# Loading q and k one at a time from batch three on, with a larger attention lead and the constants split over two engines

## The chip, the cores and the metric

The kernel runs on one core of one Trainium2 chip. The metric is the device time of one execution in microseconds (us); the time before is about 306 us. A run is called fast when it is within 1.5% of the fastest run of the same kernel in the same job, and slow otherwise. Ratios are the mean time of one kernel's fast runs over that of the other's fast runs of the same rounds, so they are not quite the ratio of the medians that are quoted beside them.

Engine names in the profile: PE is TensorE's matmul, PEld its weight load, DVE VectorE, ACT ScalarE, POOL GpSimd, SP SyncE (which here only issues DMAs). The page and the views count from the start of the span.

## The reference

Causal attention with a decay that is summed along the sequence, then an MLP mixer over tokens and channels. There are 8 batches, 8 heads, 576 positions, 64 dimensions a head.

```python
def _attn_ref(q, k, v, s):                      # q, k, v: (8, 8, 576, 64), s: (8, 8, 576)
    scores = scale * np.matmul(q, k.transpose(0, 1, 3, 2))
    cum = np.cumsum(np.maximum(s, 0.0), axis=-1)
    bias = -(cum[:, :, :, None] - cum[:, :, None, :])
    scores = np.where(causal, -1000000000.0, scores + np.minimum(bias, 0.0))
    scores = scores - np.max(scores, axis=-1, keepdims=True)
    attn = np.exp(scores)
    attn = attn / (np.sum(attn, axis=-1, keepdims=True) + 1e-09)
    return np.matmul(attn, v)

def _moe_ref(x, w_tok1, w_tok2, w_ch1, w_ch2):  # x: (8, 576, 512)
    h = np.maximum(x.transpose(0, 2, 1) @ w_tok1, 0.0) @ w_tok2      # token mixer
    u = x + h.transpose(0, 2, 1)
    h2 = np.maximum(u @ w_ch1, 0.0) @ w_ch2                          # channel mixer, 1536 wide
    return u + h2
```

The kernel computes only a band of the attention and proves in passing that this is allowed. Part of the proof is a bound on the norms of q and k: ScalarE squares and sums every q and k tile. If the proof fails, a slow general path runs; with these inputs it does not.

## The kernel before

The whole program is unrolled. The kernel describes each piece of work as an operation with its engine, its guessed duration, and what it reads and writes. A planner, plain Python in the kernel, puts the operations in order by simulating them with those guesses. Each engine then executes its own list **in the planned order, and nothing is reordered at run time**. Semaphores make the waits correct; the guesses only decide the order.

The planner's rule for when a successor may start is the piece that the argument needs (most comments in the code cuts are added here):

```python
            for u in o.users:                 # o was just placed at est on engine e
                if u.after is o:
                    rdy = est + occ           # "after" only keeps the order: start when o has issued
                elif u.alts.keys() == {"PE"} and e == "PE":
                    rdy = est + occ
                elif e in u.alts and len(u.alts) == 1 and not o.dma:
                    rdy = est + occ
                else:
                    rdy = fin                 # for a DMA: when it has landed
```

The loads of q and k. One load brings four heads of one batch, 288 KB as written in bf16. GpSimd issues it (the data are cast on the way). The ring `qkn` has six buffers. A buffer is read twice: VectorE transposes it into `kT` or `qT` for the scores, and ScalarE squares it for the proof.

```python
    r_qn = ring("qkn", 6, [128, S * 2], BF16)
    ...
    def load_p(fn, key, us, n=1):             # all of GpSimd's DMAs form one chain by "after"
        lastp[0] = P.op({"POOL": (0.68 * n, 0, fn)}, writes=key, prio=1, dma=us, after=lastp[0])
    ...
    def load_quad(src, b, qd):
        n = Buf(r_qn)
        load_p(lambda: nc.gpsimd.dma_start(
            out=n.t[:, :], in_=src[b, 4 * qd : 4 * qd + 4, :, :].rearrange("g (p r) d -> (g p) (r d)", r=R)),
            [(n, 0)], 128 * 0.19 / 16)
        return n

    def square(n, col):                       # ScalarE, lowest priority
        P.op({"ACT": (1.2, 1.6, lambda: nc.scalar.activation(
            out=junk[:, :], in_=n.t[:, :], func=AF.Square, accum_out=sq[:, col : col + 1]))},
            reads=[(n, 0)], writes=[("sq", col)], prio=60)
    ...
    def stage_qk(b, qd, which=(0, 1)):
        for i, src in list(enumerate((k, q)))[which[0] : which[-1] + 1]:
            n = load_quad(src, b, qd)
            qkn[(b, qd, i)] = n
            if b >= 2:
                square(n, (b * 2 + qd) * 2 + i)

    def stage_sq(b, qd):                      # batches one and two are loaded again, only to be squared
        for i, src in enumerate((k, q)):
            square(load_quad(src, b, qd), (b * 2 + qd) * 2 + i)
```

Batches count from zero in the code, so `b >= 2` is batch three on. From batch three on, v is loaded from SyncE's queue, and the mixer's input is transposed by DMA (`uTa<-ua` and `uTb<-ub`), also from SyncE. `LAG` sets by how much the channel mixer of a batch stands behind attention in the priorities.

## Time and profile before

Before: 307.39 us median of the first three runs (303.72 to 307.66); 305.92 us with the later one of the same job. The profiled execution has a span of 304.4 us.

| part of the span | what limits it | read from |
|---|---|---|
| 0 to 15 us | start: loads, constants, first scores; TensorE is kept busy with matmuls on zeros | slices |
| 15 to 200 us | TensorE, without a gap | slices, windows |
| 200.9 to 206.7 us | one hole: DMA transposes of batch six are late | list of waits |
| 206.7 to 298 us | TensorE, the first 6 us at a low clock | windows |
| 298 to 304 us | last addition, store, end | chain |

The head of the page of before: busy time of each engine, then the span in 40 slices (a digit is the busy share in tenths; PEclk is the granted TensorE clock in tenths).

```profile
span 304.4 us, 6438 instructions
...
PE 290.0 (95%) x2588; PEld 163.7 (54%) x2588; DVE 190.0 (62%) x403; ACT 174.3 (57%) x291; POOL 45.7 (15%) x93
...
PE   7999999999999999999999999938999999999991
...
PEclk9999999999999999999999999996999999999997
```

The list of waits of before (engine, line, what it waited for: total us, times, longest). Three lines: the hole, and the waits of the squares for their loads.

```profile
ACT junk L586 <- DMA qkn<-in_k_dram: 14.8, 4, 5.5
...
ACT junk L586 <- DMA qkn<-in_q_dram: 7.5, 4, 4.0
...
PE pmx L920 <- DMA uTb<-ub: 5.8, 1, 5.8
```

Busy time by window in before. The columns are the window, its length, busy us of PE, PEld, DVE, ACT and POOL with instruction counts, then the granted clock, DMA share and GB/s.

```profile
45.00:60.00 15.00, 15.00 (x167) 8.52 (x164) 12.04 (x26) 13.18 (x21) 2.66 (x6) 1.00 1.16 228
60.00:80.00 20.00, 20.00 (x193) 12.77 (x192) 18.00 (x39) 18.21 (x32) 2.11 (x4) 1.00 1.06 227
80.00:100.00 20.00, 20.00 (x212) 11.37 (x210) 17.96 (x41) 11.39 (x19) 1.43 (x4) 1.00 0.76 135
100.00:120.00 20.00, 20.00 (x154) 9.88 (x152) 15.33 (x32) 14.09 (x23) 1.60 (x4) 1.00 0.82 177
120.00:180.00 60.00, 59.91 (x546) 32.48 (x545) 45.02 (x96) 32.74 (x52) 4.55 (x10) 1.00 0.56 108
...
206.70:212.50 5.80, 5.78 (x57) 3.16 (x58) 4.39 (x9) 4.03 (x6) 0.00 (x0) 0.58 0.21 81
```

TensorE is full in every window from 45 to 180 us, and between 60 and 80 us ScalarE is 91% busy as well. The last line shows the clock after the hole: 0.58 over 5.8 us.

The timeline of ScalarE in before, 49 to 62 us (start, duration, operation; in brackets idle time and its end). The `junk` lines are the squares of the loads; they stand **between** the exponentials (`E<-psc`) and the evictions of the mixer.

```profile
49.41 1.16 ACT L586 ACTIVATE junk<-qkn 128x1152 bf16<-128x1152 bf16 x1
...
53.85 1.93 ACT L681 ACTIVATE E<-psc 128x1024 bf16<-128x1024 f32 x2
...
57.33 1.15 ACT L586 ACTIVATE junk<-qkn 128x1152 bf16<-128x1152 bf16 x1
...
59.77 1.92 ACT L681 ACTIVATE E<-psc 128x1024 bf16<-128x1024 f32 x2
```

### The profile page before, as it was taken

To read this page: it belongs to the slowest core of one execution; us is meant where nothing else is said; L and a number is where in the kernel's file an instruction comes from. 1 tells how busy PE (TensorE), PEld (TensorE's weight loads), DVE (VectorE), ACT (ScalarE), POOL (GpSimd) and SP (SyncE) were. 2 spreads that over 40 slices of the span, in tenths; PEclk is the share of its full clock that TensorE was granted. 3 is DMA by queue.
4 is the path that set the end of the run, shared out by engine and by line. 5 is a ranking of instruction groups with operands and counts; after the bars stand their busy time and mean duration, and the time that the engine had idled before them with its cause. 6 is when DMAs were issued, how large, how long until landed. Compare 5 with 4: busy or idle time off the path is not lost.

```text
span 304.4 us, 6438 instructions
## 1 busy us (share of the span) xinstructions
PE 290.0 (95%) x2588; PEld 163.7 (54%) x2588; DVE 190.0 (62%) x403; ACT 174.3 (57%) x291; POOL 45.7 (15%) x93
## 2 busy tenths in 40 slices
PE   7999999999999999999999999938999999999991
PEld 2478855556755454457645455414764444457540
DVE  8674848788979966978867578956617333420020
ACT  3757878998872666538732688726862065018400
POOL 8984601210001010001001012200000000000000
PEclk9999999999999999999999999996999999999997
DMA  7999999999975995892228345993003410350032
GB/s 144 199 178 260 221 210 216 236 209 256 215 142 96 196 228 113 138 210 43 41 57 162 102 79 98 136 139 88 3 2 69 115 60 1 72 141 15 3 106 75
DMA packets 58341, 38.62 MB, mean 127 GB/s; under 512 B 44480, under 2 KB 47936, under 8 KB 58304
## 3 DMA queue, kind: packets, MB, share of 16 engines
q0 software_dynamic: 10128, 17.93, 34.7%
q1 hardware_dynamic: 48176, 20.21, 29.3%
q8 instruction: 22, 0.36, 0.5%
q14 instruction: 15, 0.12, 0.1%
HBM read 40.71 MB, written 9.44 MB: 165 GB/s over the span
## 4 chain that ended last, share of the span: by engine, by line
PE 86%; DMA 5%; POOL 3%; DVE 2%; issue 1%; ACT 0%; POOLq 0%; DVEq 0%
PE pmx L920 31%; PE pmx L938 29%; PE psc L657 6%; PE pmx L829 5%; PE pav L726 5%; PE pmx L798 5%; DMA uTb<-ub 4%; DMA vf<-in_v_dram 1%; PE psc L650 1%; POOL vf L553 1%; PE psc L726 1%; PE psc L798 1%; DVE gb L929 1%; POOL qkn L580 1%; PE pmx L832 1%
## 5 line engine op out<-in xcount | busy, mean ns | idle before, releaser
L920 PEld LDWEIGHTS <-wc 128*128 128x128 bf16 x624 | 59.1, 99 | 36.4 <-issue 6.9
L681 ACT ACTIVATE E<-psc 128x1024 bf16<-128x1024 f32 x61 | 59.8, 1022 | 31.3 <-PE psc L657 30.1
L920 PE MATMUL pmx<-uTb,wc 128*128 128x320 bf16 x384 | 57.8, 305 | 5.9 <-DMA uTb<-ub 5.8
L938 PE MATMUL pmx<-wc,gb 128*128 128x512 bf16 x240 | 54.9, 379 | 0.0
L586 ACT ACTIVATE junk<-qkn 128x1152 bf16<-128x1152 bf16 x32 | 37.2, 1161 | 22.5 <-DMA qkn<-in_k_dram 14.8
L938 PE MATMUL pmx<-wc,ga 128*128 128x512 bf16 x192 | 45.2, 379 | 0.0
L920 PE MATMUL pmx<-uTa,wc 128*128 128x512 bf16 (+1 forms) x240 | 44.9, 337 | 0.2 <-ACT uTa L870 0.2
L927 ACT ACTIVATE gb<-pmx 128x320 bf16<-128x320 f32 x72 | 31.1, 437 | 22.2 <-PE pmx L920 17.1
L927 ACT ACTIVATE ga<-pmx 128x512 bf16<-128x512 f32 (+1 forms) x53 | 26.7, 506 | 20.5 <-PE pmx L920 19.2
L938 PEld LDWEIGHTS <-gb 128*128 128x128 bf16 x240 | 22.6, 98 | 25.4 <-issue 0.3
L726 PEld LDWEIGHTS <-E 128*128 128x128 bf16 x576 | 24.6, 97 | 10.9 <-issue 1.5
L566 DVE TENSOR_TENSOR vp<-vf,wT 128x512 bf16<-128x512 f32 (+1 forms) x40 | 26.3, 682 | 4.3 <-DMA vf<-in_v_dram 4.1
L736 DVE TENSOR_TENSOR x<-pav,rc 128x320 bf16<-128x320 f32 x56 | 27.4, 490 | 1.7
L732 DVE RECIPROCAL rc<-pav 128x5 f32<-128x5 f32 x56 | 10.6, 189 | 28.7 <-PE pav L726 28.5
L938 PEld LDWEIGHTS <-ga 128*128 128x128 bf16 x192 | 17.8, 98 | 19.6 <-issue 0.8
L657 PEld LDWEIGHTS <-kT 32*128 32x128 bf16 x640 | 16.6, 94 | 16.4 <-issue 13.7
L726 PE MATMUL pav<-vp,E 128*128 128x65 bf16 x504 | 24.5, 193 | 0.0
L657 PE MATMUL psc<-qT,kT 32*128 32x256 bf16 (+2 forms) x608 | 24.1, 254 | 0.0
L580 POOL DMA_DIRECT2D qkn<-in_k_dram x20 | 10.8, 541 | 85.0 <-DVE E L697 28.0
L689 DVE TENSOR_TENSOR E<-E,keep 128x512 bf16<-128x512 bf16 x48 | 19.5, 410 | 3.0 <-ACT E L681 2.8
L829 PE MATMUL pmx<-h,w 128*128 128x512 bf16 (+1 forms) x82 | 21.1, 364 | 0.0
L952 DVE TENSOR_TENSOR of<-pmx,ub 128x512 f32<-128x512 f32 x16 | 11.0, 689 | 15.9 <-PE pmx L938 12.2
(105 smaller groups left out, 257.2 us busy)
## 6 DMA issues: line engine op xcount, KB each, us to landing
out_dram<-of SPq DMA_DIRECT2D x32, 256.0 KB, 3.1
vf<-in_v_dram SPq DMA_DIRECT2D x24, 256.0 KB, 6.7
qkn<-in_k_dram POOLq DMA_DIRECT2D x20, 288.0 KB, 6.2
qkn<-in_q_dram POOLq DMA_DIRECT2D x20, 288.0 KB, 5.8
vf<-in_v_dram POOLq DMA_DIRECT2D x8, 256.0 KB, 7.6
wc<-in_moe_w_ch_dram POOLq DMA_DIRECT2D x4, 384.0 KB, 9.3
wc<-in_moe_w_ch_dram POOLq DMA_DIRECT2D x3, 512.0 KB, 11.3
out_dram<-of SPq DMA_DIRECT2D x8, 128.0 KB, 2.4
```

Of the source, the lines that this page charges most:

```text
L566: eng.tensor_tensor(out=vp.t[p0 : p0 + n, c, :, 0:D], in0=vf.t[p0 : p0 + n, c, :, :], in1=wT[p0 : p0 + n, cw, b * H : b * H + H].unsqueeze ...
L586: P.op({"ACT": (1.2, 1.6, lambda: nc.scalar.activation(out=junk[:, :], in_=n.t[:, :], func=AF.Square, accum_out=sq[:, col : col + 1]))}, r ...
L657: nc.tensor.matmul(out=pss[g // 2].bank(g % 2)[:, o], lhsT=kT.t[rows, j0 : j0 + 128, e], rhs=qT.t[rows, a:z, e], start=(e == 0 and not fol ...
L681: nc.scalar.activation(out=E.t[:, :, gi * 512 : gi * 512 + 512], in_=ps.t[:, :, :], func=AF.Exp, scale=0.125)
L689: nc.vector.tensor_tensor(out=o, in0=o, in1=keep[:, :].unsqueeze(1).unsqueeze(1).to_broadcast([128, 2, 2, 128]), op=ALU.mult)
L726: nc.tensor.matmul(out=o[:, i, ic, 0 : D + 1], lhsT=E.t[:, hh, d0 : d0 + 128], rhs=vp.t[:, jc, h + hh, 0 : D + 1], start=(jc == j_lo), sto ...
L736: nc.vector.tensor_tensor(out=x.t[:, :, h0 * D : (h0 + n) * D].rearrange("p c (e d) -> p e c d", e=n), in0=view()[:, :, :, 0:D], in1=rc.t[ ...
L798: nc.tensor.matmul(out=pm()[:, (ha - h0) * D : (hb - h0) * D], lhsT=w1[:, NJ if odd and c == NJ - 1 else c, t * 128 : t * 128 + 128], rhs= ...
L829: nc.tensor.matmul(out=pm.t[:, 0 : e - a], lhsT=w2[:, t, w0 : w0 + 128], rhs=h1.t[:, t, a:e], start=(t == 0), stop=(t == NTC - 1 and b not ...
L920: nc.tensor.matmul(out=pm.t[:, 0 : e - a], lhsT=wc1[:, m, cc * 128 : cc * 128 + 128], rhs=uT.t[:, m, a:e], start=(m == 0), stop=(m == NMC ...
L927: lambda cc=cc, pm=pm, a=a, e=e: nc.scalar.activation(out=g.t[:, cc, a:e], in_=pm.t[:, 0 : e - a], func=AF.Relu),
L938: nc.tensor.matmul(out=pm.t[:, :], lhsT=g.t[:, cc, c * 128 : c * 128 + 128], rhs=wc2[:, cc, :], start=(cc == 0), stop=(cc == NCC - 1 and b ...
```

## The change

The intent. The hole at 201 us comes when q/k loads and DMA transposes share the DMA engines, so the change thins out the loads: GpSimd copies one element of the load before, which makes its queue wait until that load has landed. It also tells the planner that the DMA transposes land 1.2 us later than it believed, raises `LAG` from 2 to 3, makes the constants with two GpSimd selects and VectorE instead of GpSimd alone, splits the last output tile in two halves, and moves a few PSUM choices of batch one. The core of the diff:

```diff
+            o.slow = slow                                     # in op()
-                fin = dma_free + (1.5 if e == "POOL" else 0.9)
+                fin = dma_free + (1.5 if e == "POOL" else 0.9) + o.slow
...
-    LAG = 2.0
+    LAG = 3.0
...
+    nc.vector.memset(ident[:, :], 0.0)
+    nc.vector.memset(keep[:, :], 0.0)
     def consts():
-        make_identity(nc, identf)
-        make_identity(nc, ident)
-        make_upper_triangular(nc, keep, val=1.0, diag=True)
+        nc.gpsimd.affine_select(out=ident[:, :], in_=ident[:, :], ...)
+        nc.gpsimd.affine_select(out=keep[:, :], in_=keep[:, :], ...)
     def negs():                                               # negs2() likewise
-            nc.gpsimd.tensor_scalar(out=negm[:, a : a + w], in0=keep[:, 0:w], ...)
+            nc.vector.tensor_scalar(out=negm[:, a : a + w], in0=keep[:, 0:w], ...)
...
+    held = [None]
     def load_quad(src, b, qd):
         n = Buf(r_qn)
+        if held[0] is not None:
+            lastp[0] = P.op({"POOL": (0.12, 0.2, lambda h=held[0]: nc.gpsimd.tensor_copy(
+                out=gate[0:1, 0:1], in_=h.t[0:1, 0:1]))}, reads=[(held[0], 0)], writes=["held"], prio=1, after=lastp[0])
+        if b >= 2:
+            held[0] = n
         load_p(lambda: nc.gpsimd.dma_start(
...
                     P.op({"SP": (1.25, 0, trd)}, reads=rk, writes=[(uT, c, 0)],
-                         prio=0, dma=0.5)
+                         prio=0, dma=0.5, slow=1.2)
...
+            for (d0, d1) in ((0, DM // 2), (DM // 2, DM)) if last_c else ((0, DM),):   # last output tile in halves
```

Left out: the halved matmuls, additions and stores of that last loop, the order of v's first loads, and the PSUM choices.

The copy reads the load before (`reads=[(held[0], 0)]`): it waits until the load has landed.

More of the change, by code (lines that the diff above doesn't have):

```diff
@@ L57, in __init__, with op @@
         self.readers = {}
-    def op(self, alts, reads=(), writes=(), prio=0, dma=0.0, holds=(), after=None):
+    def op(self, alts, reads=(), writes=(), prio=0, dma=0.0, holds=(), after=None, slow=0.0):
         o = Op()
+        o.slow = slow
         o.alts = alts
@@ L366 @@
     FOLD = ((0, 0), (0, 1), (1, 0), (1, 1))
-    AV2 = ()
     PEADD = (0, 1)
@@ L441, in consts @@
     def consts():
-        make_identity(nc, identf)
-        make_identity(nc, ident)
-        make_upper_triangular(nc, keep, val=1.0, diag=True)
+        nc.gpsimd.affine_select(out=ident[:, :], in_=ident[:, :], compare_op=ALU.not_equal, fill=1.0, base=0,
+                                pattern=[[-1, 128]], channel_multiplier=1)
+        nc.gpsimd.affine_select(out=keep[:, :], in_=keep[:, :], compare_op=ALU.is_gt, fill=1.0, base=0,
+                                pattern=[[-1, 128]], channel_multiplier=1)
     def negs():
+        nc.vector.tensor_copy(out=identf[:, :], in_=ident[0:64, 0:64])
         for a, w in ((0, 128), (256, 128), (448, 64)):
-            nc.gpsimd.tensor_scalar(out=negm[:, a : a + w], in0=keep[:, 0:w], scalar1=30000.0, scalar2=-30000.0,
+            nc.vector.tensor_scalar(out=negm[:, a : a + w], in0=keep[:, 0:w], scalar1=30000.0, scalar2=-30000.0,
                                     op0=ALU.mult, op1=ALU.add)
@@ L452, in negs2 @@
         for a, w, k0 in ((0, 128, 0), (256, 128, 0), (448, 64, 64)):
-            nc.gpsimd.tensor_scalar(out=nego[:, a : a + w], in0=keep[:, k0 : k0 + w], scalar1=30000.0, scalar2=-30000.0,
+            nc.vector.tensor_scalar(out=nego[:, a : a + w], in0=keep[:, k0 : k0 + w], scalar1=30000.0, scalar2=-30000.0,
                                     op0=ALU.mult, op1=ALU.add)
     def load_consts():
-        lastp[0] = P.op({"POOL": (1.3, 1.5, consts)}, writes=["const"], prio=0, after=lastp[0])
-        lastp[0] = P.op({"POOL": (0.7, 0.9, negs)}, reads=["const"], writes=["negm"], prio=0, after=lastp[0])
+        lastp[0] = P.op({"POOL": (0.6, 0.8, consts)}, writes=["const"], prio=0, after=lastp[0])
+        P.op({"DVE": (0.5, 0.7, negs)}, reads=["const"], writes=["negm", "identf"], prio=-4)
+        P.op({"DVE": (0.4, 0.6, negs2)}, reads=["const"], writes=["nego"], prio=5)
     def pads(eng, i):
@@ L519, in w_tr @@
                                     identity=identf[:, :])
-        P.op({"PE": (0.7, 1.1, w_tr)}, reads=["wn", "const"], writes=[(bw, 0)], prio=(0,))
+        P.op({"PE": (0.7, 1.1, w_tr)}, reads=["wn", "identf"], writes=[(bw, 0)], prio=(0,))
         P.op({**dve(384, lambda: nc.vector.tensor_copy(out=wT[:, :, :].rearrange("p c e -> p (c e)"), in_=bw.t[:, 0:384])),
@@ L557, in stage_v @@
             else:
-                load_p(load, [(vf, c)], 1024 * 0.02 / 16 * n / 128, 1.5)
+                load_p(load, [(vf, c)], (0.75 if b or c == 0 else 1.25) * n / 128, 1.4)
                 yield
@@ L638, in quad @@
             fold = (b, qd) in FOLD
-            pss = [Duo() if b == 0 and qd * 4 + gi * 2 + e in (2, 5, 7) else Solo(r_sc) for e in range(2)]
+            pss = [Duo() if b == 0 and qd * 4 + gi * 2 + e in (2, 5) else Solo(r_sc) for e in range(2)]
             c0 = 0
@@ L709, in pair @@
         vkeys = [(vp, c) for c in range(NJ)] + [(vp, "w")] + (["padv"] if b == 1 else [])
-        for hs in ([(0, 1)] if b == 0 else [(0,), (1,)]):
-            pa = Solo(r_sc if b == 0 else r_mx if b in AV2 and hs[0] else r_av)
+        for hs in ([(0, 1)] if b == 0 and np_ != 1 else [(0,), (1,)]):
+            pa = Solo(r_sc if b == 0 and np_ != 1 else r_mx if b == 0 else r_av)
             rc = Buf(r_rc, False)
@@ L933, in chan @@
         for ci, c in enumerate((4, 0, 1, 2, 3) if odd else (0, 1, 2, 3)):
-            pm, o = Buf(r_mx, False), Buf(r_o, False)
-            for th in range(3):
-                def mm(c=c, pm=pm, th=th):
-                    for cc in range(th * 4, th * 4 + 4):
-                        nc.tensor.matmul(out=pm.t[:, :], lhsT=g.t[:, cc, c * 128 : c * 128 + 128], rhs=wc2[:, cc, :],
-                                         start=(cc == 0), stop=(cc == NCC - 1 and b not in OADD))
-                    if b in OADD and th == 2:
-                        sr, ii = (us, 0) if c == NJ - 1 else (u, c)
-                        nc.tensor.matmul(out=pm.t[:, :], lhsT=ident[:, :], rhs=sr.t[:, ii, :], start=False, stop=True)
-                P.op({"PE": (4 * c_pe(512)[0], 4 * c_pe(512)[0] + 0.3, mm)}, reads=gkeys + [("wc2", th)],
-                     writes=[(pm, 0)], holds=[o], prio=(rank + 2.0 + 2.0 * ci / NJ, 1))
+            o = Buf(r_o, False)
             if odd:
@@ L949, in chan @@
             sk = ukeys[(us, 0, 0)] + ukeys[(us, 0, 64)] if src is us else ukeys[(u, si, 0)]
-            def add(pm=pm, o=o, src=src, si=si):
-                nc.vector.tensor_tensor(out=o.t[:, :], in0=pm.t[:, :], in1=src.t[:, si, :], op=ALU.add)
-            if b in OADD:
-                P.op(either(512, lambda pm=pm, o=o: nc.scalar.copy(out=o.t[:, :], in_=pm.t[:, :]),
-                            lambda pm=pm, o=o: nc.vector.tensor_copy(out=o.t[:, :], in_=pm.t[:, :])),
-                     reads=[(pm, 0)] + sk, writes=[(o, 0)], prio=0)
-            else:
-                P.op(dve(512, add), reads=[(pm, 0)] + sk, writes=[(o, 0)], prio=0)
@@ L960, in st, with mm, add @@
-            def st(o=o, c=c):
-                if c < NJ - 1:
-                    nc.sync.dma_start(out=out[b, c * 128 : c * 128 + 128, :], in_=o.t[:, :])
-                else:
-                    for i in range(2):
-                        nc.sync.dma_start(out=out[b - 1 + i, NQ:S, :], in_=o.t[i * 64 : i * 64 + 64, :])
-            P.op({"SP": (0.45 if c < NJ - 1 else 0.9, 0, st)}, reads=[(o, 0)], prio=0.5, dma=128 * 0.088 / 16)
+            last_c = b == B - 1 and ci == NJ - 1
+            for (d0, d1) in ((0, DM // 2), (DM // 2, DM)) if last_c else ((0, DM),):
+                pm = Buf(r_mx, False)
+                for th in range(3):
+                    def mm(c=c, pm=pm, th=th, src=src, si=si, d0=d0, d1=d1):
+                        for cc in range(th * 4, th * 4 + 4):
+                            nc.tensor.matmul(out=pm.t[:, 0 : d1 - d0], lhsT=g.t[:, cc, c * 128 : c * 128 + 128],
+                                             rhs=wc2[:, cc, d0:d1],
+                                             start=(cc == 0), stop=(cc == NCC - 1 and b not in OADD))
+                        if b in OADD and th == 2:
+                            nc.tensor.matmul(out=pm.t[:, :], lhsT=ident[:, :], rhs=src.t[:, si, :], start=False, stop=True)
+                    occ = 4 * c_pe(d1 - d0)[0]
+                    P.op({"PE": (occ, occ + 0.3, mm)}, reads=gkeys + [("wc2", th)] + (sk if b in OADD and th == 2 else []),
+                         writes=[(pm, 0)], holds=[o], prio=(rank + 2.0 + 2.0 * ci / NJ, 1))
+                def add(pm=pm, o=o, src=src, si=si, d0=d0, d1=d1):
+                    nc.vector.tensor_tensor(out=o.t[:, d0:d1], in0=pm.t[:, 0 : d1 - d0], in1=src.t[:, si, d0:d1], op=ALU.add)
+                if b in OADD:
+                    P.op(either(512, lambda pm=pm, o=o: nc.scalar.copy(out=o.t[:, :], in_=pm.t[:, :]),
+                                lambda pm=pm, o=o: nc.vector.tensor_copy(out=o.t[:, :], in_=pm.t[:, :])),
+                         reads=[(pm, 0)] + sk, writes=[(o, 0)], prio=0)
+                else:
+                    P.op(dve(d1 - d0, add), reads=[(pm, 0)] + sk, writes=[(o, d0)], prio=0)
+                def st(o=o, c=c, d0=d0, d1=d1):
+                    if c < NJ - 1:
+                        nc.sync.dma_start(out=out[b, c * 128 : c * 128 + 128, d0:d1], in_=o.t[:, d0:d1])
+                    else:
+                        for i in range(2):
+                            nc.sync.dma_start(out=out[b - 1 + i, NQ:S, :], in_=o.t[i * 64 : i * 64 + 64, :])
+                P.op({"SP": (0.45 if c < NJ - 1 else 0.9, 0, st)}, reads=[(o, d0)], prio=0.5,
+                     dma=128 * 0.088 / 16 * (d1 - d0) / DM)
@@ L974 @@
     stage_qk(0, 1, (0,))
-    next(sv)
     load_consts()
     weights()
+    next(sv)
     stage_qk(0, 1, (1,))
@@ L986 @@
         load_ch1(1, m2)
-    if any(b == 1 for (b, qd) in FOLD):
-        lastp[0] = P.op({"POOL": (0.8, 1.0, negs2)}, reads=["const"], writes=["nego"], prio=0, after=lastp[0])
     for i in range(2):
```

## The prediction

> **What bounds it now.** TensorE: 290.0 of 304.4 us busy (the page's engine shares), full from 15 to 298 us except one hole. The list of waits names it: the channel mixer's first matmul on uTb waited 5.8 us for DMA uTb<-ub. There four q/k loads (issued 189 to 195 us, as buffers come free) share the DMA engines with batch six's five DMA transposes; these land 7 to 12 us after issue, against 2.4 alone. After the hole the granted clock is 0.58 from 206.7 to 212.5 us (the window table): 2.4 us more. This fits the Trainium skill, "TensorE: Matmul & The Clock Gate", Part 1: an idle window of about 3.4 us halves the clock. The hole costs about 8 us.
>
> **Gains.** (1) Hole: the eight late loads that only feed the norm check move ahead of those transposes: 6 to 8 us. They are not really throttled: all read the same, long landed tile. (2) Start: three memsets (0.6 us) and the -30000 masks (0.77 + 0.77 us) leave GpSimd; v's later issues come earlier: at most 1 us. (3) End: the last output is split; last add 0.69 to about 0.4 us, last store 3.1 to about 2.5: 0.5 to 1 us. Matmul columns are unchanged apart from 0.9 us more filler.
>
> **The cost.** The wait is a GpSimd copy reading the load before, in an in-order queue, so from batch three only one q/k load is in flight. In before, the first six such loads were in flight together behind the w_ch2 load; each took 12.4 to 14.6 us but they landed about 1.5 us apart, 45.7 to 53.6 us. The skill's "DMA: Bandwidth & Descriptors", Anatomy of one DMA, gives about 2.0 us fixed plus the transfer; serialized, the fixed part is paid each time. The trace agrees but is higher: a lone 288 KB load takes 3.6 to 3.8 us from issue to landing (140 to 180 us), 5.9 to 6.6 while the v loads run (45 to 89 us). With some 0.5 us for wait, copy and reissue, one load takes 4.2 to 6.8 us.
>
> That is on the critical path: ScalarE is in order and its squares of these loads stand between exponentials and evictions. The sixth load's square stands before batch three's second pair of exponentials: earliest 45.7 + 5 x 4.2 = 67 us, about 73 with v traffic; in before those ran at 59.8. The twelfth load (square at 79.8): earliest 92, likelier 100 to 106. ScalarE (91% busy, 60 to 80 us) and three PSUM buffers leave no slack, so TensorE stalls in pieces, some long enough to lower the clock. The larger attention lead makes these loads more urgent. From about 110 us loads are sparse and nothing is lost or regained.
>
> Sum (span): 304.4 - 8 (hole) - 1.5 (ends) + 22 (12 to 30) + 2 (clock) = 319; timed runs stand some 2 us above the span, within the error. **Predicted 319 us, 80% between 307 and 331. Faster 0.08, same 0.14, slower 0.78.**
>
> **What would show it.** GpSimd waiting on DMA qkn for most of 45 to 110 us, one q/k load every 4 to 7 us; squares waiting for DMA qkn over 15 us more in sum; TensorE below 80% busy in 50 to 110 us; that stretch's work ending 15 to 28 us later; the uTb wait under 2 us, the clock near 1.0 there.
>
> **What would make it wrong.** If loads land near 3.6 us despite v traffic, or TensorE has more slack than it seems, the loss shrinks to the gain: about 307; if the waits were not effective, about 296.

## The result

333.31 us median of 4 runs (331.73 to 334.06) against 305.92 us (303.72 to 307.66): the ratio is 1.0893, 95% interval 1.0794 to 1.0991. (As everywhere here, the ratio is the mean of the fast runs of one kernel over that of the other's fast runs of the same rounds, so not quite the ratio of the two medians.) The change makes the kernel 9% slower. The profiled run has a span of 330.0 us.

The head of the page after:

```profile
span 330.0 us, 6511 instructions
...
PE 296.0 (90%) x2605; PEld 167.0 (51%) x2605; DVE 195.2 (59%) x421; ACT 170.6 (52%) x284; POOL 51.2 (16%) x114
...
PE   6999997187967799879997999999999999999992
...
PEclk9999998769987999999999999999999999999998
```

The hole at 201 us is gone, and TensorE now has gaps from the seventh slice (50 us) to the 22nd (180 us). TensorE is busy for 6.0 us more although its matmuls are the same but for a few more on zeros (26 in the trace against 21, 0.3 us of busy time); the clock is lower in slices 7 to 13.

The list of waits after:

```profile
POOL gate L588 <- DMA qkn<-in_k_dram: 57.0, 12, 12.0
POOL gate L588 <- DMA qkn<-in_q_dram: 49.3, 12, 6.0
...
ACT junk L598 <- DMA qkn<-in_q_dram: 27.3, 9, 5.3
ACT junk L598 <- DMA qkn<-in_k_dram: 24.1, 9, 6.0
...
DVE qT L642 <- DMA qkn<-in_q_dram: 6.4, 3, 3.5
DVE kT L642 <- DMA qkn<-in_k_dram: 6.1, 3, 5.4
```

The squares now wait 51.4 us for their loads (27.3 + 24.1), against 22.3 us in before; VectorE's transposes wait 12.5 us. No wait on uTb stands in the list any more.

The same windows after:

```profile
45.00:60.00 15.00, 11.61 (x106) 7.03 (x101) 6.61 (x13) 4.79 (x10) 2.63 (x6) 0.89 0.93 185
60.00:80.00 20.00, 10.68 (x82) 5.28 (x82) 9.53 (x21) 11.65 (x18) 3.37 (x9) 0.74 0.55 96
80.00:100.00 20.00, 16.81 (x150) 10.26 (x149) 14.66 (x33) 11.34 (x20) 3.24 (x10) 0.90 0.89 170
100.00:120.00 20.00, 16.09 (x178) 10.07 (x177) 13.64 (x34) 13.03 (x21) 3.25 (x11) 0.93 0.56 96
120.00:180.00 60.00, 54.96 (x504) 29.20 (x503) 44.10 (x94) 31.36 (x47) 7.93 (x20) 1.00 0.69 138
...
200.00:220.00 20.00, 20.00 (x180) 9.91 (x180) 17.26 (x33) 13.59 (x20) 5.98 (x15) 1.00 0.73 137
```

Between 60 and 80 us TensorE is busy for 10.7 us of 20, at a mean clock of 0.74, and the DMA engines are half idle (share 0.55 against 1.06). So the DMA engines have room; the run with two loads in flight, below, tests whether a second load would use it.

GpSimd's timeline after shows one turn of the new loop: the copy waits for the landing, then the next load is issued.

```profile
60.16 0.18 POOL L588 COPY gate<-qkn 1x1 bf16<-1x1 bf16 x1 [6.36 <-DMA qkn<-in_k_dram]
60.67 0.54 POOL L592 DMA_DIRECT2D qkn<-in_q_dram  x1 [0.33 <-issue]
64.94 0.18 POOL L588 COPY gate<-qkn 1x1 bf16<-1x1 bf16 x1 [3.73 <-DMA qkn<-in_q_dram]
65.45 0.53 POOL L592 DMA_DIRECT2D qkn<-in_k_dram  x1 [0.34 <-issue]
```

And ScalarE's timeline after, at the place that was shown for before:

```profile
60.12 1.16 ACT L598 ACTIVATE junk<-qkn 128x1152 bf16<-128x1152 bf16 x1 [5.96 <-DMA qkn<-in_k_dram]
...
64.90 1.16 ACT L598 ACTIVATE junk<-qkn 128x1152 bf16<-128x1152 bf16 x1 [3.53 <-DMA qkn<-in_q_dram]
...
66.06 1.92 ACT L693 ACTIVATE E<-psc 128x1024 bf16<-128x1024 f32 x2
...
74.69 1.16 ACT L598 ACTIVATE junk<-qkn 128x1152 bf16<-128x1152 bf16 x1 [3.39 <-DMA qkn<-in_q_dram]
```

The first exponentials of batch three ran at 53.85 us before and run at 66.06 us now. In front of them stands the square of the fourth load, which waits for that load.

### The profile page after: what moved, and what is told of

It is laid out like the page before. It is cut to its first block, busy times and chain, and to the rows that moved or that the text cites. A ratio compares the mean times of both kernels' runs of the same rounds, so it can differ in the third digit from the quotient of the medians.

```text
span 330.0 us, 6511 instructions
## 1 busy us (share of the span) xinstructions
PE 296.0 (90%) x2605; PEld 167.0 (51%) x2605; DVE 195.2 (59%) x421; ACT 170.6 (52%) x284; POOL 51.2 (16%) x114
## 4 chain that ended last, share of the span: by engine, by line
PE 60%; DMA 23%; issue 7%; DVE 3%; ACT 3%; POOL 2%; POOLq 0%; ACTq 0%
PE pmx L958 25%; PE pmx L932 21%; DMA qkn<-in_q_dram 10%; DMA vf<-in_v_dram 5%; DMA qkn<-in_k_dram 5%; PE pmx L841 4%; PE pmx L810 4%; PE psc L669 3%; DMA wc<-in_moe_w_ch_dram 3%; PE pav L738 3%; ACT E L693 2%; ACT junk L598 1%; POOL qkn L592 1%; DVE gb L941 1%; DVE of L968 1%
## 5 line engine op out<-in xcount | busy, mean ns | idle before, releaser
L693 ACT ACTIVATE E<-psc 128x1024 bf16<-128x1024 f32 x62 | 60.8, 1021 | 39.0 <-PE psc L669 37.7
L932 PE MATMUL pmx<-uTb,wc 128*128 128x320 bf16 x384 | 59.3, 306 | 7.8 <-ACT gb L939 7.8
L598 ACT ACTIVATE junk<-qkn 128x1152 bf16<-128x1152 bf16 x32 | 37.2, 1163 | 51.4 <-DMA qkn<-in_q_dram 27.3
L958 PE MATMUL pmx<-wc,gb 128*128 128x512 bf16 (+1 forms) x252 | 54.6, 369 | 0.2 <-DVE ua L852 0.2
L958 PE MATMUL pmx<-wc,ga 128*128 128x512 bf16 x192 | 47.6, 398 | 0.0
L939 ACT ACTIVATE gb<-pmx 128x320 bf16<-128x320 f32 x70 | 30.0, 437 | 22.8 <-PE pmx L932 18.5
L958 PEld LDWEIGHTS <-gb 128*128 128x128 bf16 x252 | 23.6, 98 | 24.7 <-issue 0.8
L958 PEld LDWEIGHTS <-ga 128*128 128x128 bf16 x192 | 18.7, 102 | 22.3 <-issue 4.1
L939 ACT ACTIVATE ga<-pmx 128x512 bf16<-128x512 f32 (+1 forms) x47 | 23.3, 506 | 12.3 <-PE pmx L932 11.5
L642 DVE STREAM_TRANSPOSE kT<-qkn 128x576 f32<-128x576 f32 x16 | 20.0, 1252 | 8.4 <-DMA qkn<-in_k_dram 6.1
L588 POOL COPY gate<-qkn 1x1 bf16<-1x1 bf16 x31 | 8.1, 260 | 106.4 <-DMA qkn<-in_k_dram 57.0
L642 DVE STREAM_TRANSPOSE qT<-qkn 128x576 f32<-128x576 f32 x16 | 20.0, 1248 | 6.5 <-DMA qkn<-in_q_dram 6.4
```

Source lines behind the costliest of these rows:

```text
L598: P.op({"ACT": (1.2, 1.6, lambda: nc.scalar.activation(out=junk[:, :], in_=n.t[:, :], func=AF.Square, accum_out=sq[:, col : col + 1]))}, r ...
L642: P.op({"DVE": (1.24, 1.4, lambda n=n, dst=dst: nc.vector.transpose(out=dst.t[:, 0:S, :].rearrange("d t e -> d (t e)").bitcast(FP32).rearr ...
L693: nc.scalar.activation(out=E.t[:, :, gi * 512 : gi * 512 + 512], in_=ps.t[:, :, :], func=AF.Exp, scale=0.125)
L932: nc.tensor.matmul(out=pm.t[:, 0 : e - a], lhsT=wc1[:, m, cc * 128 : cc * 128 + 128], rhs=uT.t[:, m, a:e], start=(m == 0), stop=(m == NMC ...
L939: lambda cc=cc, pm=pm, a=a, e=e: nc.scalar.activation(out=g.t[:, cc, a:e], in_=pm.t[:, 0 : e - a], func=AF.Relu),
L958: nc.tensor.matmul(out=pm.t[:, 0 : d1 - d0], lhsT=g.t[:, cc, c * 128 : c * 128 + 128], rhs=wc2[:, cc, d0:d1], start=(cc == 0), stop=(cc == ...
```

## The experiments

The theory: in a fixed order, one load in flight cannot bring the tiles as early as ScalarE's and VectorE's lists ask for them, and every late tile stops TensorE. Rivals: the larger lead or the moved constants spoil the order; the copies delay other work in GpSimd's queue; one load at a time is too slow in any order.

Medians below are of all runs of a kernel. Before ran in every job: medians 306.10, 305.78 and 306.33 us, single runs from 300.03 to 311.48. In the job of the first four runs before's fastest run was 300.03 us, so only the few runs near it count as its fast ones and the ratios of that job are rough (their intervals say so); there the medians are the better guide. Before also spreads more than the kernels without the hole (`e_nowait`: 299.99 to 301.26), and its mean clock differs from run to run (0.998 in the run of 300.03 us, 0.992 or less in the others of that job). So the hole is perhaps not the same in every execution; only one execution of before was profiled, so this is not shown.

### The wait alone, and all but the wait

Two edits. `e_nowait` is the changed kernel without these lines:

```diff
-        if b >= 2:
-            held[0] = n
```

> The changed kernel without the wait: q/k loads are issued as buffers come free, everything else of the change stays. Theory (the one-at-a-time loads cost the time, and the rest of the change gains a little): 295 to 301 us, no TensorE hole over 2 us between 45 and 180 us. Rival (the larger attention lead or the moved constants made the order of work worse, and the waits only show it): 320 us or more.

`e_waitonly` is the kernel before with the copy (the same five added lines of `load_quad` as in the change) and nothing else.

> The kernel before with the wait alone added, lead 2, old constants, old tail. Theory: 325 to 337 us, squares waiting for DMA qkn in 45 to 120 us as in the changed kernel. Rival (larger lead and new order are to blame): 303 to 310 us.

Measured: without the wait 300.67 us median (299.99 to 301.26; ratio 0.9964, interval 0.9819 to 1.0108); the wait alone 336.00 us (334.71 to 337.82; ratio 1.112, interval 1.0938 to 1.1303). Both as the theory said. The lead and the constants are not to blame: the whole loss comes with the wait, and without it the change is about 5 us faster than before by the medians (the interval of the ratio does not exclude a tie). In the wait alone the squares wait 53.7 us for their loads (34.5 + 19.2), and the wait does not even close the hole that it was meant for. This line stands in the list of waits of `e_waitonly`:

```profile
PE pmx L927 <- DMA uTb<-ub: 3.8, 1, 3.8
```

Without the wait no such line is left. So something else in the change closes the hole. In `e_nowait` the last q/k load is issued at 190.5 us, before batch six's first transpose at 193.8 us; in before two of those loads were issued after the first transpose. Which of the edits brought this order was not tested alone.

The run without the wait executes the same instructions in the same order on every engine as the changed kernel, apart from the copies. So the two traces can be laid side by side. Its list of waits has no single wait of TensorE over 2 us, and its windows are full again; these are two of them:

```profile
60.00:80.00 20.00, 20.00 (x201) 12.39 (x201) 17.76 (x43) 16.76 (x28) 2.11 (x4) 1.00 1.04 217
80.00:100.00 20.00, 19.85 (x229) 11.98 (x229) 19.50 (x48) 14.64 (x22) 1.43 (x4) 1.00 0.74 134
```

The spans are 298.7 and 330.0 us: the wait costs 31.3 us. TensorE is busy 288.6 and 296.0 us. So 7.4 us of the 31.3 are the same matmuls taking longer, and 23.9 us are gaps.

### Two in flight

The same wait, on the load before the last one, so that two are in flight:

```diff
-    held = [None]
+    held = [None, None]
...
-            held[0] = n
+            held[:] = [held[1], n]
```

> The changed kernel, where each load waits for the one before the last: two in flight. Theory (it is the rate of loads): a load every 2.3 to 3.5 us, the sixth lands by 60 us and the twelfth by 78 us, so ScalarE's waits on DMA qkn fall below 20 us in sum and the time is 296 to 305 us. Rival (any wait in GpSimd's queue delays, through the small copies for v' that stand in the same queue): still 315 us or more.

Measured: 299.38 us median (299.05 to 300.31). But this edit changes two things. The copy now reads one load and stands `after` another, so the planner's rule gives it the landing: the planner now knows of the wait and orders the work accordingly. The next run takes that away again, with the copy held to the buffer instead of reading it in the planner's books (the copy itself, and its wait on the chip, stay):

```diff
-  reads=[(held[0], 0)], writes=["held"], prio=1, after=lastp[0])
+  holds=[held[0]], writes=["held"], prio=1, after=lastp[0])
```

> Two loads in flight, the planner not told (same order on ScalarE, VectorE and TensorE as in the changed kernel and in the run without the wait; in the first run with two in flight the planner happened to know of the wait, so that run changed two things). Theory (the rate of loads against a fixed order): a load every 2.5 to 3.3 us from 46 us, sixth load landed at 57 to 61 us (its square was at 56.8 without the wait, 74.4 with one in flight), twelfth by 74 to 79 us (78.3 and 105.9): 300.5 to 305 us. Rival (in the first run with two in flight the gain over one came from the planner's knowledge, as in the run where it knew of single loads): 312 us or more.

Measured: 304.12 us median (303.16 to 305.43). This kernel has the same order on TensorE, VectorE, ScalarE and SyncE as the changed kernel and as the run without the wait, so three kernels differ only in the number of loads in flight. The start of some squares on ScalarE, in us, from the timelines:

| square of load | buffers the only limit (`e_nowait`) | two in flight (`e_two_blind`) | one in flight (after) | after minus first |
|---|---|---|---|---|
| 1 (batch three) | 47.27 | 47.95 | 47.02 | -0.3 |
| 4 | 51.68 | 53.68 | 64.90 | 13.2 |
| 6 | 57.03 | 60.51 | 74.69 | 17.7 |
| 12 (batch five) | 78.56 | 81.63 | 106.16 | 27.6 |
| 18 | 109.91 | 111.48 | 140.24 | 30.3 |
| 22 (batch eight) | 145.21 | 147.66 | 176.50 | 31.3 |
| median time of the kernel | 300.67 | 304.12 | 333.31 | 32.6 |

The delay of the last column ends at the difference of the spans, 31.3 us. Going through ScalarE's instructions one by one in the two traces, every step of the delay of 0.8 us or more stands at a square. Two in flight take away nine tenths of the loss at the same order. That settles the rival of the copies too: this kernel has the same kind of copies in the same queue.

### One in flight, but the planner knows

The changed kernel, with the copy no longer tied to the load by `after`, so that the planner sees the landing. The loads are still one at a time.

```diff
-  reads=[(held[0], 0)], writes=["held"], prio=1, after=lastp[0])
+  reads=[(held[0], 0)], writes=["held"], prio=1)
```

> The changed kernel, where the kernel's own planner is told that the copy waits for the landing (the same loads, still one at a time; only the planned order of the other engines follows it). Theory A (the cost is an order planned as if the wait took no time; with the wait known the four loads of a batch need 4 x 4.5 = 18 us of about 33 us a batch): 299 to 310 us. Theory B (one load at a time is too slow for the kernel in any order): 320 us or more, with the same sum of waits on DMA qkn.

Measured: 305.32 us median (305.10 to 307.38). Theory A. GpSimd waits almost as long as in the changed kernel (47.3 + 44.5 us, against 57.0 + 49.3 us), but the squares wait only 9.2 us (6.6 + 2.6) instead of 51.4 us. From its list of waits:

```profile
POOL gate L588 <- DMA qkn<-in_k_dram: 47.3, 10, 11.7
POOL gate L588 <- DMA qkn<-in_q_dram: 44.5, 11, 5.7
...
ACT junk L598 <- DMA qkn<-in_k_dram: 6.6, 6, 3.0
...
ACT junk L598 <- DMA qkn<-in_q_dram: 2.6, 3, 1.2
```

The loads come no earlier: the twelfth lands at 116.3 us here and at 106.1 us in the changed kernel. Only the order around them is another. One load at a time is nearly fast enough for this kernel; it is not fast enough for an order that was planned as if the wait took no time. What is left of the gap to 300 us is largely a new idle stretch of TensorE of 3.2 us between 200 and 220 us, which I did not follow further.

### Which reader carries the delay

The squares only serve the proof. They were taken out for batches three to eight (the proof is then incomplete; `sq` is zeroed, and the output of these inputs is right).

```diff
-            if b >= 2:
-                square(n, (b * 2 + qd) * 2 + i)
```

> The changed kernel, waits kept, but without ScalarE's squares of batches three to eight (the norm check is then incomplete on purpose; the output of these inputs does not need it). In the changed kernel the loads reach VectorE's transposes 9 to 10 us later than in before (fourth to eighth load), but reach the squares up to 27 us later (twelfth load: lands at 106 us, squared at 78.5 to 79.8 us in before). Theory S (the squares, in ScalarE's order ahead of exponentials and evictions, carry most of the delay): 306 to 316 us. Theory T (the transposes need the loads as late anyway): 322 us or more.

Measured: 313.94 us median (313.21 to 315.20; ratio 1.0302, interval 1.0244 to 1.0361). So of the 32.6 us between the medians of the changed kernel and the run without the wait, 19.4 us go away with the squares and 13.3 us stay. What stays is most likely the transposes that the scores need, which wait 13.9 us for loads there (7.1 + 6.8). Most of the delay passed through work that could have been done at any time, only because it stands in an in-order list. Caution: without the squares the planner also finds a somewhat different order, and ScalarE has 24 squares of 1.16 us less to do, which by itself may save time, so the split is not exact.

### The wait from batch five on

```diff
-        if b >= 2:
+        if b >= 4:
```

> The changed kernel with the wait from batch five on in place of batch three: 8 of the 24 waits fewer, and the first eight loads are issued as buffers come free. Theory (the loss is a lead that is lost while w_ch2 and the first v loads fill the queues, 45 to 80 us, after which one load per 4.5 us would keep up): 298 to 305 us. Rival (one load at a time is too slow at any stage): 312 us or more.

Measured: 308.92 us median of four runs, 304.45 and 307.78 us for the two that count as fast (ratio 1.004, interval 0.9958 to 1.0123). Between the two ranges, so both statements missed. Letting the first eight loads go free takes away most of the loss, but not all: one load at a time still costs some 4 to 7 us in the fast runs against 300.67 us.

### The lead and the start

The old lead of 2, without the wait:

```diff
-    LAG = 3.0
+    LAG = 2.0
```

> The changed kernel without the wait and with the old lead of 2: what the larger lead does by itself, beside the run without the wait (300.67 us median). If the lead matters to the hole before batch six's channel mixer: 303 us or more, with a uTb wait of over 2 us; if only the planner's longer landing time for transposes closed it: 299 to 302 us.

Measured: 301.65 us median (300.87 to 302.61; ratio 0.9900, interval 0.9845 to 0.9956), and no wait on uTb. The lead is not what closed the hole, and it is worth about 1 us at most.

Two in flight with the old constants (the memsets and masks back on GpSimd, the old order of v's first loads):

> Two loads in flight as in the earlier run (299.38 us median), with the constants made as in before (GpSimd memsets and masks, old order of v's loads). In the runs without the wait the first channel mixer matmul started at 27.3 us against 26.1 in before: theory, the new start costs about 1.2 us, so 297.7 to 298.7 us here; rival, the first 30 us do not set the end: 299 to 300 us.

Measured: 299.84 us median (299.17 to 301.82; ratio 0.9849, interval 0.9801 to 0.9897): no difference to the new constants that these runs can tell. The test was less clean than planned. The first channel mixer matmul started at 28.26 us here, against 27.57 us with the new constants and no wait and 26.33 us in before, so the old constants alone do not bring back the earlier start of before. The theory's 297.7 to 298.7 us was missed.

### The hole of the kernel before

The eight loads that only feed the proof (`stage_sq`) were left out of the kernel **before**, again incomplete:

```diff
-    for b in range(2):
-        for qd in range(2):
-            stage_sq(b, qd)
```

> The kernel before without the eight q/k loads of batches one and two that only feed the norm check (incomplete on purpose). Theory (the hole of 5.8 us before batch six's channel mixer, with the low clock after it, comes from these loads standing in front of its DMA transposes): no wait on uTb over 1 us, clock 1.00 in 200 to 220 us, 296 to 300 us. Rival (the transposes are late because of the output stores or the order of work): the hole stays, 303 us or more.

Measured: 298.60 us median (298.25 to 298.73; ratio 0.9800, interval 0.9728 to 0.9871). The wait for DMA uTb is down to 0.2 us in sum, and the windows that held the hole are full, at full clock:

```profile
200.00:206.70 6.70, 6.70 (x81) 4.48 (x80) 5.74 (x13) 4.02 (x7) 0.00 (x0) 1.00 0.31 98
206.70:212.50 5.80, 5.80 (x66) 4.43 (x64) 2.81 (x9) 3.94 (x9) 0.00 (x0) 1.00 0.01 3
```

In before, the five DMA transposes between 190 and 202 us took 7.3 to 11.8 us from issue to landing. Here they take 2.5 to 4.0 us. The hole goes with those loads, so the reading that the change starts from was right. The run also takes eight squares off ScalarE (1.16 us each) and lets the planner order the rest anew, which these numbers do not separate.

### A version that beats both

Two loads in flight, with the planner knowing, once more with five rounds:

> The first run with two in flight and the planner knowing, again, for the comparison and as the version to keep: 299 to 300.5 us, beside 304 to 307 us of before.

Measured: 299.56 us median (299.10 to 300.09), before 306.33 us; ratio 0.9829, interval 0.9776 to 0.9882. Its squares wait 8.7 us for loads (5.0 + 3.7), the transposes under 1 us, and no wait on uTb is in its list. It is a little over 2% faster by the medians and 1.7% by the ratio of fast runs; at a threshold of 2% that verdict is unclear. It is the best complete kernel, ahead of the run without any wait by 1.1 us between the medians of two jobs, which is too little to claim.

## Why the prediction was right or wrong

It said slower with 0.78, and the kernel is slower; but 333.3 us lies outside 307 to 331 us. The mechanism was right and terms of the sum were mis-sized: in spans, the profiled run took 330.0 us where the sum said 319. Of these 11 us, some 7 are a loss that was put too low (24 for 31.3 us) and some 4 a gain that was put too high (9.5 for 5.7 us).

- **What bounds before: right.** TensorE and one hole. The run without the eight loads shows both the cause of the hole and its worth: 306.33 to 298.60 us, 7.7 us, where I wrote "about 8 us" (that run also dropped eight squares, as said there).
- **Gains of 9.5 us (8 for the hole, 1.5 for the ends): too high.** Everything but the wait brought the span from 304.4 to 298.7 us, 5.7 us. The end gained about 0.4 us: 6.4 us from the last matmul to the end of the span in before, 6.0 us without the wait. The start gained nothing: the first channel mixer matmul came at 27.57 us, 1.2 us later than in before. Why it came later stays open: with the old constants and two loads in flight it came at 28.26 us.
- **One load takes 4.2 to 6.8 us: right.** From the second load's issue at 46.12 us to the thirteenth's at 106.71 us there are 11 turns, 5.5 us each on average. The first two took 7.1 and 7.4 us, above the range, and the other nine 5.1 us on average, so the middle of the range was met partly by luck.
- **When the tiles come: right within 2 us.** I expected the sixth load's square at "about 73" and the twelfth's likelier at "100 to 106" us. In the changed kernel they started at 74.69 and 106.16 us.
- **The loss of "22 (12 to 30)" + 2 us: this is the step that failed. It measured 31.3 us.** Two faults. First, I did not draw the conclusion from my own line above. The twelfth square at 100 to 106 us against 79.8 us is a delay of 20 to 26 us (and 79.8 us was a miscount: in before that is the eleventh square, the twelfth ran at 81.77 us); the right comparison was the same order without the wait, where that square stands at 78.56 us, so the delay is 27.6 us. I wrote 22. Second, "From about 110 us loads are sparse and nothing is lost or regained" is false by half: nothing was regained, but the delay grew from 27.6 to 30.3 us at load 18 and to 31.3 us at load 22. The order leaves almost no slack between landing and square there even without the wait (in `e_nowait` the square of load 18 starts 0.1 us after its landing), so any later landing shows in full.
- **The low clock: named, but counted too low.** I put 2 us. TensorE's busy time grew by 7.4 us against the run without the wait, with a mean clock of 0.74 between 60 and 80 us. The gaps alone, 23.9 us, are close to the 22 us of the sum. TensorE's account (gaps and longer matmuls) and the delay of the squares are two ways to count the same 31.3 us, so the clock should not have been a term of its own: in the list of ScalarE's instructions the delay grows by steps of 0.8 us or more only at squares that wait for a load, and the slow matmuls run between them.
- **Signs.** GpSimd waiting on DMA qkn for most of 45 to 110 us: yes, 48 us of 65 (106 us in the whole run). One load every 4 to 7 us: yes but for the first two turns. Squares waiting over 15 us more: yes, 29.1 us more. TensorE below 80% from 50 to 110 us: yes, 69% in the mean (41.5 of 60 us, summed over windows of 10 us). That stretch's work 15 to 28 us later: yes, 27.6 us at the twelfth square, the upper end. uTb wait gone and clock near 1.0 there: yes, though not because of the wait, as `e_nowait` and `e_waitonly` show.
- **What I had not seen** is the way out: I took the late order as given by the loads. It was given by one `after`. With the planner knowing, the same single load in flight costs 5 us instead of 33.

## What to carry to other kernels

A throttle on loads is a wait, and a wait has to stand in the model that sets the order: here the same wait cost 33 us when the planner believed that it took no time, and about 5 us when it knew. Before serializing loads, divide the time between two needs of consecutive tiles by the full turn of one load (issue, landing, wait, next issue; here 5.5 us, of which GpSimd worked for about 0.7), and keep at least two in flight if the quotient is near one. Work that nobody waits for, such as a check, still delays everything behind it when it stands early in an in-order list and its input is late.

## What the Trainium skill lacked or had wrong

- "DMA: Bandwidth & Descriptors", section Anatomy of one DMA: it fits about 2.0 us plus bytes over 436 GB/s, but does not say which bytes count for a load that casts. The q/k load writes 288 KB (an estimate by that fit: 2.7 us) and reads twice that in fp32 (estimate: 3.4 us); alone it took 3.6 to 3.8 us in before. The bytes read fit better; no run here varies the bytes to test it.
- Same page: I found no figure there for what a load costs when each waits for the one before in GpSimd's queue. Here the turn was 5.5 us a load on average, with about 0.33 us between the end of the waiting copy and the next issue.
- No page that I read gives a figure for how much ordinary loads delay DMA transposes beside them: 2.4 us from issue to landing alone, 7.3 to 11.8 us with q/k loads in front.
- "TensorE: Matmul & The Clock Gate", Part 1: it says that the clock halves after an idle window of about 3.4 us. Before agrees: after a gap of 5.8 us the clock averaged 0.58 over the next 5.8 us. The changed kernel does not fit so simply: the clock was also at 0.50 from 56 to 58 us after a gap of only 2.45 us (51.44 to 53.88 us), and from 98 to 102 us after one of 3.19 us, while it stayed at 1.00 after gaps of 2.22, 2.84 and 2.04 us (at 105.6, 139.2 and 177.9 us). Why these differ is not shown. For a kernel with many short stalls the runs add a size: 7.4 us of longer matmuls beside 23.9 us of gaps.
